# Loading q and k a batch ahead around the batch change of an attention and mixer kernel

## Chip, cores and metric

One core of one Trainium2 chip. The metric is the device time of one execution in microseconds (us). A profiled execution has a span some 1.8 us shorter than its time (434.77 us of time for 433.0 us of span).

## The reference, cut to what matters

```python
# q, k, v: (batch 8, heads 8, seq 576, head_dim 64), fp32
scores = scale * q @ k.transpose(0, 1, 3, 2) + bias[head]        # relative-position bias
attn   = exp(scores - max) ;  attn /= attn.sum(-1) + 1e-09
x      = (attn @ v) as (batch, seq, 512)                         # heads side by side
u      = x + ((x.T @ U) @ V).T                                   # low-rank mix over seq
out    = u + relu(u @ w_ch1) @ w_ch2                             # 512 -> 2048 -> 512
```

## The kernel before

Each batch is four *groups* (a pair of heads each), so there are 32, numbered 0 to 31; `g` is the group, `b` its batch, `pr` its slot in the batch. From group 4 on a group has three *thirds* (`seg`), each with score matmuls, the work of the pair before, and a ration of matmuls of an earlier batch's 512-2048-512 layer that fills TensorE's time. Scores need q and k with head_dim on the partitions. Batches 0 and 1 are transposed on TensorE; batches 2 to 7 are loaded by POOL as 128-row tiles (cast to bf16 on the way) and transposed by DMA, issued on SP, into `qkT[b % 2]`:

```python
    def hold(due, g, out, in_):
        held.append((due, g, lambda: nc.sync.dma_start_transpose(out=out, in_=in_)))

    def load_tasks(b, lag=2):                      # 15 items
        g0 = b * NPAIR
        def main(which, t):
            tl = load_main(b, which, t)            # POOL DMA
            if which < 2:                          # q, k: a transpose two thirds later
                hold(now[0] + lag, g0, qkT[b % 2][:, :, which, cols], tl)
        ...
        # order: remainder rows of q, k; q0 k0 q1 k1 q2 k2 q3 k3; remainder rows of v; v0..v3

    def emit_held(g, seg):                         # at the start of each third
        now[0] = 3 * g + seg
        ...                                        # at most two transposes that are due
...
    for g in range(NPAIR, NG):
        b, pr = divmod(g, NPAIR)
        for seg in range(3):
            emit_held(g, seg)
            ...                                    # scores of this third
            if seg == 1 and b < B - 1 and pr:
                if pr == 1:
                    pool_order += load_tasks(b + 1)
                # gate: POOL waits here until pair g - 1 is normalised
                nc.gpsimd.tensor_copy(out=gate, in_=x_pr[g - 1][0:1, 0, 0:2])
            if pr:
                for _ in range(3):
                    if pool_order:
                        pool_order.pop(0)()
            work.run(...)
            ...
```

So all 15 loads of the next batch, and ten transposes, fall into the last three groups of the batch before it. SP is one queue in order, and also carries the transposes of the mixer's input (`uT<-u_tok`) and the stores.

At the start, the four pairs of batch 0 come by plain loads in fp32: the first two pairs on SP and ScalarE, the third and fourth on SP at 10.9 to 14.6 us, between loads of the bias table. POOL casts the third, issues eight loads, and casts the fourth.

The softmax here doesn't subtract the row's maximum and nothing guards it: scores larger than these inputs give would overflow.

Of the kernel before, what the change touches and what calls it, by code (L numbers as in the profile page):

```python
# [35 lines left out]
def kernel(  # L36
# [12 lines left out]
    nc = tc.nc  # L49
    B, H, S, D = q.shape  # L50
# [9 lines left out]
    SP = 640  # L60
    S0 = 512
    P4W = 704
    NPAIR = H // 2
# [32 lines left out]
    gate = const.tile([1, 2], BF16)  # L96
# [4 lines left out]
    qkT = [const.tile([128, NPAIR, 2, SP], BF16, name=f"qkT{i}") for i in range(2)]  # L101
# [16 lines left out]
    def rem_heads(t):  # L118
        return t.rearrange("p (a two d) -> p a two d", two=2, d=D)
# [31 lines left out]
    def setup_gm():  # L151
        nc.vector.tensor_scalar(
            out=negt31, in0=tblT[:, 31:32], scalar1=-1.0, scalar2=None, op0=ALU.mult
        )
        nc.scalar.activation(gmT, tblT, AF.Exp, bias=negt31, scale=1.0)
# [69 lines left out]
    def first_load(which, h0, h1, st, dma):  # L225
        dma.dma_start(
            out=st.rearrange("p (h x) -> p h x", h=h1 - h0),
            in_=(q, k)[which][0, h0:h1, 0:S0, :].rearrange(
                "h (p j) d -> p h (j d)", j=4
            ),  # L230
        )

    def first_cast(st, cast):
        qb = qbp.tile([128, 512], BF16, name="qb")
        cast(  # L235
            out=qb.rearrange("p (j h d) -> p h j d", j=4, h=2),
            in_=st.rearrange("p (h j d) -> p h j d", h=2, j=4),
        )
        return qb

    def load_main(b, which, t):
        src = (q, k, v)[which]
        if which < 2:
            tl = qbp.tile([128, 512], BF16, name="qb")
            dst = tl.rearrange("p (h d) -> p h d", h=H)
        else:
            tl, dst = None, v_bf[b % 2][:, t, :, 0:64]
        nc.gpsimd.dma_start(  # L248
            out=dst,
            in_=src[b, :, t * 128 : (t + 1) * 128, :].rearrange("h p d -> p h d"),  # L250
        )
        return tl

    def load_pair(which, pr):
        tl = qbp.tile([128, 512], BF16, name="qb")
        dst = tl.rearrange("p (j h d) -> p j h d", j=4, h=2)
        for hh in range(2):
            nc.gpsimd.dma_start(  # L258
                out=dst[:, :, hh, :],
                in_=(q, k)[which][1, 2 * pr + hh, 0:S0, :].rearrange(  # L260
                    "(t p) d -> p t d", p=128
                ),
            )
        return tl

    def load_rem(b, which):
        src = (q, k, v)[which]
        vr = src[b, :, S0:S, :].rearrange("(a two) p d -> two p a d", two=2)
        if which < 2:
            dst = rem_heads(rem[b % 2][which])  # L270
        else:
            dst = v4_bf[b % 2].rearrange("p (a two) c -> p a two c", two=2)
        for par in range(2):
            rows = slice(par * 64, par * 64 + 64)
            nc.gpsimd.dma_start(out=dst[rows, :, par, 0:64], in_=vr[par])

    held = []
    now = [0]

    def hold(due, g, out, in_):  # L280
        held.append((due, g, lambda: nc.sync.dma_start_transpose(out=out, in_=in_)))  # L281

    def load_tasks(b, lag=2):
        g0 = b * NPAIR

        def main(which, t):
            tl = load_main(b, which, t)
            if which < 2:
                cols = slice(t * 128, (t + 1) * 128)
                hold(now[0] + lag, g0, qkT[b % 2][:, :, which, cols], tl)  # L290

        def remt(which):
            load_rem(b, which)
            if which < 2:
                src = rem[b % 2][which]
                hold(now[0] + lag, g0, qkT[b % 2][:, :, which, S0:SP], src)

        seq = [lambda which=which: remt(which) for which in range(2)]
        for t in range(NKT):
            for which in range(2):  # L300
                seq.append(lambda which=which, t=t: main(which, t))
        seq.append(lambda: remt(2))
        for t in range(NKT):
            seq.append(lambda t=t: main(2, t))
        return seq

    def load_uv():
        nc.gpsimd.dma_start(
            out=upad[:, 0:4, 0:R],
            in_=moe_U[0:S0, :].rearrange("(t p) r -> p t r", p=128),  # L310
        )
        for par in range(2):
            rows = slice(par * 64, par * 64 + 64)
            nc.gpsimd.dma_start(out=upad[rows, 4 + par, 0:R], in_=moe_U[S0:S, :])
        nc.gpsimd.dma_start(out=vpad[0:R, 0:S], in_=moe_V)

    def load_w1(ct):
        nc.gpsimd.dma_start(
            out=w1b[:, ct, :], in_=moe_w_ch1[ct * 128 : (ct + 1) * 128, :]
        )  # L320
# [187 lines left out]
    def band(g, kt):  # L508
        pr = g % NPAIR
        if kt < NKT:  # L510
            q0 = max(0, 128 * kt - 128)
            q1 = min(S, 128 * kt + 256)
            d0 = q0 - (128 * kt - 128)
            t = p_sb[g % 2][:, kt, :, q0:q1]
            e = eb[:, 2 * pr : 2 * pr + 2, d0 : d0 + q1 - q0]
        else:
            t = p4_sb[g % 2][:, 384:SP]
            e = eb4[:, pr, :]
        nc.vector.tensor_tensor(out=t, in0=t, in1=e, op=ALU.mult)  # L519
# [37 lines left out]
    x_pr = {}  # L557
# [61 lines left out]
    def mix_ut(g):  # L619
        mix_ut_ps(g)()  # L620
# [46 lines left out]
    qk0 = {}  # L667
    pool_cast = nc.gpsimd.tensor_copy
# [4 lines left out]
    q2, k2 = scratch[:, 1024:1536], scratch[:, 1536:2048]  # L673
    q3, k3 = scratch[:, 2048:2560], scratch[:, 2560:3072]
    first_load(0, 0, 2, q00, nc.sync)
    first_load(1, 0, 2, k00, nc.scalar)
    first_load(0, 2, 4, q1, nc.sync)
    first_load(1, 2, 4, k1, nc.scalar)
    nc.scalar.activation(gmT[:, 0:1], negt31, AF.Exp)
    setup_gm()  # L680
    setup_gp()
    load_eb(4)
    load_eb(0)
    first_load(0, 4, 6, q2, nc.sync)
    first_load(1, 4, 6, k2, nc.sync)
    load_eb(1)
    first_load(0, 6, 8, q3, nc.sync)
    first_load(1, 6, 8, k3, nc.sync)
# [11 lines left out]
    qk0[1] = [first_cast(x, nc.scalar.copy) for x in (q1, k1)]  # L700

    load_uv()
    load_rem(1, 0)
    load_rem(1, 1)
    qk0[2] = [first_cast(x, pool_cast) for x in (q2, k2)]
    qk1 = [[load_pair(which, 0) for which in range(2)]]
    for i in range(4):
        load_w1(i)
    qk0[3] = [first_cast(x, pool_cast) for x in (q3, k3)]
    load_rem(1, 2)  # L710
    for t in range(NKT):
        load_main(1, 2, t)
# [109 lines left out]
    pool_order = []  # L822
# [4 lines that stand above are left out]
            box = []  # L827
            if seg:
                main_scores(g, 2 * seg - 2)
            else:  # L830
                box = remainder_scores(g)
            if seg == 1 and b < B - 1 and pr:
                if pr == 1:
                    pool_order += load_tasks(b + 1)
                nc.gpsimd.tensor_copy(out=gate, in_=x_pr[g - 1][0:1, 0, 0:2])  # L835
            if pr:
                for _ in range(3):
                    if pool_order:
                        pool_order.pop(0)()
            work.run(1.85 if g < 2 * NPAIR + 2 else 2.2)  # L840
            for p in box:
                p()
            if g == NPAIR:
                if seg == 0:
                    pv(g - 1, 2)
                    pv(g - 1, 3)
                    normalise(g - 1)
                elif seg == 1:
                    mix_t(g - 1, nc.vector.tensor_copy)
                    mix_ut(g - 1)  # L850
                    ready[0] = True
                    work.run(1.5)
            elif seg == 0:
                if g > NPAIR + 1:
                    mix_h(g - 2)
            elif seg == 2:
                mix_t(g - 1, nc.scalar.copy)
            if seg == 0:
                band(g, 4)
                if NPAIR < g < 2 * NPAIR:  # L860
                    put_off.pop(0)()
                    put_off.pop(0)()
                if g > NPAIR:
                    pv_head(g - 1, 0)
            elif seg == 1:
                if g + 1 < 2 * NPAIR:
                    second_transposes(g + 1, qk1[g + 1 - NPAIR], 0)
                band(g, 0)
                band(g, 1)
                if g > NPAIR:  # L870
                    pv_head(g - 1, 1)
                if b > 1 and pr == 1:
                    ready[b - 1] = True
            else:
                if g + 1 < 2 * NPAIR:
                    second_transposes(g + 1, qk1[g + 1 - NPAIR], 1)
                band(g, 2)
                band(g, 3)
    g = NG - 1

    def last_rem(g):
# [46 lines left out]
```

## Time and profile before

| | before |
|---|---|
| time, first three runs | 431.82 us (431.15 to 433.02) |
| time of the run that was profiled | 434.77 us (span 433.0) |
| TensorE busy | 395.2 us, 91% |
| group length, undisturbed, from group 10 | 10.46 us |
| five batch changes (waiting group and the next) | 21.3 us above two undisturbed groups each |

The prediction shows the page's shares, the windows at the batch changes and the SP timeline. In the rows of a timeline, the time in square brackets is how long the engine stood idle before the instruction, and after the arrow stands what ended that.

### The profile page before, as it was taken

How to read it: one execution, taken by the hardware profiler on the slowest of the kernel's cores; microseconds unless marked ns; L12 is line 12 of the kernel's file. 1: busy time of each engine (PE TensorE's matmuls, PEld its weight loads, DVE VectorE, ACT ScalarE, POOL GpSimd, SP SyncE). 2: the span in 40 equal slices, each digit the busy share in tenths (PEclk: the TensorE clock that was granted, in tenths of full speed). 3: DMA queues.
4: the chain of work that ended last, by engine and by line, in shares of the span. 5: the costliest groups of instructions: out<-in, count | busy, mean ns of one | idle time of the engine just before them, and what ended most of it. 6: DMA issues, size and time to landing. Idle time of an engine off the chain costs nothing.

```text
span 433.0 us, 8998 instructions
## 1 busy us (share of the span) xinstructions
PE 395.2 (91%) x3620; PEld 212.7 (49%) x3620; DVE 241.4 (56%) x545; ACT 204.5 (47%) x283; POOL 126.7 (29%) x184
## 2 busy tenths in 40 slices
PE   2868988999969996999989998999699999999995
PEld 1545455555525553455545553555355554444442
DVE  5786877557715675356855674557455662331421
ACT  4867444566624554355545563456455651120310
POOL 8787475019200750038104810183000000000000
PEclk9899999999969999899999998999999999999998
DMA  9999999519961999139924993199812102101013
GB/s 152 227 182 141 144 161 156 116 55 140 141 64 62 110 124 139 39 74 157 155 38 75 174 134 53 54 138 159 85 38 69 44 15 63 58 2 73 26 24 73
DMA packets 167553, 42.56 MB, mean 98 GB/s; under 512 B 157232, under 2 KB 162392, under 8 KB 167512
## 3 DMA queue, kind: packets, MB, share of 16 engines
q0 software_dynamic: 108128, 17.39, 61.4%
q1 hardware_dynamic: 58840, 24.08, 28.9%
q8 instruction: 28, 0.46, 0.4%
q10 hardware_dynamic: 544, 0.52, 0.4%
q14 instruction: 13, 0.11, 0.1%
HBM read 37.84 MB, written 9.45 MB: 109 GB/s over the span
## 4 chain that ended last, share of the span: by engine, by line
PE 80%; DMA 8%; DVE 3%; SPq 3%; POOL 2%; issue 2%; ACT 1%; ACTq 0%; DVEq 0%
PE acc L356 30%; PE acc L341 26%; PE o L543 9%; PE sc L456 7%; DMA qkT<-qb 5%; SPq L281 2%; PE acc L579 2%; PE acc L595 2%; PE sc L469 2%; PE sc L490 1%; DMA g<-in_q_dram 1%; DMA tblT<-in_bias_table_dram 1%; POOL qb L235 1%; POOL qb L258 1%; DVE g L352 1%
## 5 line engine op out<-in xcount | busy, mean ns | idle before, releaser
L465 ACT ACTIVATE p_sb<-sc 128x1024 bf16<-128x1024 f32 x128 | 124.3, 1022 | 106.9 <-PE sc L456 106.6
L356 PE MATMUL acc<-w2b,g 128*128 128x512 bf16 x576 | 136.3, 387 | 0.0
L341 PE MATMUL acc<-uT,w1b 128*128 128x512 bf16 x512 | 121.2, 384 | 0.1
L356 PEld LDWEIGHTS <-g 128*128 128x128 bf16 x576 | 54.5, 99 | 73.1 <-issue 15.0
L341 PEld LDWEIGHTS <-w1b 128*128 128x128 bf16 x576 | 53.7, 98 | 72.7 <-issue 14.9
L352 DVE TENSOR_SCALAR g<-acc 128x512 bf16<-128x512 f32 x92 | 63.3, 690 | 44.0 <-PE acc L341 42.9
L519 DVE TENSOR_TENSOR p_sb<-p_sb,eb 128x768 bf16<-128x768 bf16 (+3 forms) x160 | 70.9, 467 | 12.9 <-ACT p_sb L465 12.2
L543 PEld LDWEIGHTS <-p_sb 128*128 128x128 bf16 x1600 | 55.8, 98 | 8.3 <-issue 2.0
L350 ACT ACTIVATE g<-acc 128x512 bf16<-128x512 f32 x52 | 31.1, 598 | 60.5 <-PE acc L341 44.2
L543 PE MATMUL o<-v_bf,p_sb 128*128 128x65 bf16 x1500 | 58.0, 193 | 0.0
L835 POOL COPY gate<-xp 1x2 bf16<-1x2 bf16 x18 | 3.2, 176 | 155.4 <-DVE xp L568 155.4
L366 DVE TENSOR_TENSOR ob<-acc,u_tok 128x512 f32<-128x512 f32 x32 | 22.1, 691 | 46.9 <-PE acc L356 46.6
L456 PE MATMUL sc<-qkT 64*128 64x512 bf16 x256 | 41.5, 392 | 1.4 <-ACT p_sb L482 0.6
L603 DVE TENSOR_TENSOR u_tok<-acc,xp 128x512 bf16<-128x512 f32 x32 | 22.0, 689 | 30.2 <-PE acc L595 30.0
L568 DVE TENSOR_TENSOR xp<-o,rcp 128x320 bf16<-128x320 f32 x60 | 29.5, 491 | 3.2
L469 PE MATMUL sc<-qkT 128*128 128x128 bf16 x128 | 14.4, 223 | 17.7 <-DMA qkT<-qb 13.8
L482 ACT ACTIVATE p_sb<-sc 128x512 bf16<-128x512 f32 x32 | 19.1, 597 | 24.2 <-PE sc L645 19.7
L248 POOL DMA_DIRECT2D v_bf<-in_v_dram x32 | 28.6, 912 | 4.7 <-PE acc L579 1.9
L248 POOL DMA_DIRECT2D qb<-in_k_dram x24 | 22.2, 923 | 3.0 <-issue 1.5
L248 POOL DMA_DIRECT2D qb<-in_q_dram x24 | 22.6, 940 | 0.3 <-DMA rem<-in_q_dram 0.3
L499 ACT ACTIVATE p_sb<-sc 128x640 bf16<-128x640 f32 x32 | 22.4, 699 | 0.1
L469 PEld LDWEIGHTS <-qkT 128*128 128x128 bf16 x128 | 8.9, 98 | 20.7 <-DMA qkT<-qb 15.2
(82 smaller groups left out, 250.2 us busy)
## 6 DMA issues: line engine op xcount, KB each, us to landing
out_dram<-ob SPq DMA_DIRECT2D x32, 256.0 KB, 2.0
v_bf<-in_v_dram POOLq DMA_DIRECT2D x32, 128.0 KB, 9.8
qb<-in_q_dram POOLq DMA_DIRECT2D x24, 128.0 KB, 5.5
qb<-in_k_dram POOLq DMA_DIRECT2D x24, 128.0 KB, 6.4
w1b<-in_moe_w_ch_dram POOLq DMA_DIRECT2D x4, 512.0 KB, 8.8
w2b<-in_moe_w_ch_dram POOLq DMA_DIRECT2D x4, 512.0 KB, 10.2
out_dram<-ob SPq DMA_DIRECT2D x8, 128.0 KB, 2.3
g<-in_q_dram SPq DMA_DIRECT2D x3, 256.0 KB, 6.3
```

The costliest lines, as they stand in the source:

```text
L248: nc.gpsimd.dma_start(out=dst, in_=src[b, :, t * 128 : (t + 1) * 128, :].rearrange("h p d -> p h d"),)
L341: nc.tensor.matmul(gp_, lhsT=w1b[:, ct, nt * 128 : (nt + 1) * 128], rhs=rhs[:, ct, :], start=(ct == 0), stop=(ct == 3),)
L350: nc.scalar.activation(g[:, nt, :], gp_, AF.Relu)
L352: nc.vector.tensor_relu(out=g[:, nt, :], in_=gp_)
L356: nc.tensor.matmul(op, lhsT=g[:, nt, tt * 128 : (tt + 1) * 128], rhs=w2b[:, nt, :], start=(nt == 0), stop=(nt == NHT - 1),)
L456: nc.tensor.matmul(sp[:, hh, :], lhsT=kT[rows, i * 128 : (i + 1) * 128], rhs=qT[rows, 0:S0], start=True, stop=True,)
L465: nc.scalar.activation(P[:, i, :, 0:S0], sp, AF.Exp, scale=scale)
L469: nc.tensor.matmul(sp[:, 0, kt * 128 : (kt + 1) * 128], lhsT=kT[:, kt * 128 : (kt + 1) * 128], rhs=qT[:, S0:SP], start=(kt == 0), stop=(kt ...
L499: nc.scalar.activation(P4[:, 0:SP], sp.rearrange("p a c -> p (a c)")[:, 0:SP], AF.Exp, scale=scale,)
L519: nc.vector.tensor_tensor(out=t, in0=t, in1=e, op=ALU.mult)
L543: nc.tensor.matmul(o[:, qt * 66 : qt * 66 + 65], lhsT=lhs[:, c0 : c0 + 128], rhs=rhs, start=(kt == NKT and qt == 0), stop=(kt == NKT - 1), ...
L568: nc.vector.tensor_tensor(out=xo[:, :, hh], in0=o[:, :, 0:64], in1=rbc, op=ALU.mult)
```

## The change

Its intent: take the transposes' landing off TensorE's path at each batch change. Loads of q and k begin a batch ahead (five items in the last slot of the batch before the last one, five in the next first slot), the transposes are due from the second slot's second third on, two a third, and v is loaded in the third slot. Batch 2, which cannot begin so early, gets five items in group 5 and ten in group 6. At the start the third pair's loads go to ScalarE's queue, and POOL casts pairs three and four ahead of the weights.

```diff
-    def load_tasks(b, lag=2):
+    def load_tasks(b):
         g0 = b * NPAIR
+        due = max(3 * (g0 - 3) + 1, now[0] + 2)
...
-                hold(now[0] + lag, g0, qkT[b % 2][:, :, which, cols], tl)
+                hold(due, g0, qkT[b % 2][:, :, which, cols], tl)
...
     first_load(1, 2, 4, k1, nc.scalar)
+    first_load(0, 4, 6, q2, nc.scalar)
+    first_load(1, 4, 6, k2, nc.scalar)
     nc.scalar.activation(gmT[:, 0:1], negt31, AF.Exp)
...
-    first_load(0, 4, 6, q2, nc.sync)
-    first_load(1, 4, 6, k2, nc.sync)
...
+    qk0[2] = [first_cast(x, pool_cast) for x in (q2, k2)]
     load_rem(1, 0)
     load_rem(1, 1)
-    qk0[2] = [first_cast(x, pool_cast) for x in (q2, k2)]
+    qk0[3] = [first_cast(x, pool_cast) for x in (q3, k3)]
+    load_w1(0)
+    load_w1(1)
     qk1 = [[load_pair(which, 0) for which in range(2)]]
-    for i in range(4):
-        load_w1(i)
-    qk0[3] = [first_cast(x, pool_cast) for x in (q3, k3)]
+    load_w1(2)
+    load_w1(3)
...
-            if seg == 1 and b < B - 1 and pr:
-                ...                                  (three items a third, as above)
+            if seg == 1 and g > NPAIR:
+                n = 0
+                if g == NPAIR + 1:
+                    pool_order += load_tasks(2)
+                    n = 5
+                elif g == NPAIR + 2:
+                    n = 10
+                elif pr == 3 and b < B - 2:
+                    pool_order += load_tasks(b + 2)
+                    n = 5
+                elif pr == 0 and b < B - 1:
+                    n = 5
+                elif pr == 2 and b < B - 1:
+                    n = 5
+                if n:
+                    nc.gpsimd.tensor_copy(out=gate, in_=x_pr[g - 1][0:1, 0, 0:2])
+                    for _ in range(n):
                         pool_order.pop(0)()
```

Source lines move by one after the first edit: L469 before is L470 after, L611 is L612.

More of the change, by code (lines that the diff above doesn't have):

```diff
@@ L295, in remt @@
                 src = rem[b % 2][which]
-                hold(now[0] + lag, g0, qkT[b % 2][:, :, which, S0:SP], src)
+                hold(due, g0, qkT[b % 2][:, :, which, S0:SP], src)
         seq = [lambda which=which: remt(which) for which in range(2)]
@@ L831 @@
                 box = remainder_scores(g)
-            if seg == 1 and b < B - 1 and pr:
-                if pr == 1:
-                    pool_order += load_tasks(b + 1)
-                nc.gpsimd.tensor_copy(out=gate, in_=x_pr[g - 1][0:1, 0, 0:2])
-            if pr:
-                for _ in range(3):
-                    if pool_order:
+            if seg == 1 and g > NPAIR:
[15 more added lines that the diff above has]
+                    for _ in range(n):
                         pool_order.pop(0)()
@@ L878 @@
                 band(g, 3)
+    assert not pool_order and not held
     g = NG - 1
```

## The prediction

> **What bounds the kernel now.** I read the page first (engine shares, slices), then the PE timeline around each batch change, then the windows over those stretches, then the SP and POOL timelines that feed them.
>
> ```profile
> PE 395.2 (91%) x3620; PEld 212.7 (49%) x3620; DVE 241.4 (56%) x545; ACT 204.5 (47%) x283; POOL 126.7 (29%) x184
> PE   2868988999969996999989998999699999999995
> PEclk9899999999969999899999998999999999999998
> DMA  9999999519961999139924993199812102101013
> ```
>
> TensorE is the bound: 91% busy, nothing else over 56%. So time can only come from TensorE's idle time (433.0 - 395.2 = 38 us) and from stretches at a lower clock. The idle time sits in the first slices and in single dents every fourth group, and each dent follows slices in which the DMA engines are full. The program works in groups (one pair of heads each, four to a batch, 0 to 31); inside the dents are the batch changes. The windows from the first score matmul of a batch to the last that had to wait (columns: length, PE busy, clock, DMA):
>
> ```profile
> core 0: us, PE busy (x), PEclk, DMA share, GB/s
> 120.66:124.84 4.18, 0.50 (x6) 0.79 1.06 106
> 168.90:173.30 4.40, 0.71 (x8) 1.00 1.27 151
> 216.79:218.35 1.56, 0.40 (x8) 1.00 0.63 120
> 259.86:262.44 2.58, 0.56 (x7) 1.00 0.99 163
> 305.63:309.57 3.94, 0.57 (x7) 1.00 1.25 117
> ```
>
> These are batches 3 to 7. In 16.7 us TensorE works 2.7, so about 13.9 us are waits. What they wait for, in the PE timeline, and what comes after, in the windows of the following group:
>
> ```profile
> 124.84 0.29 PE L469 MATMUL sc<-qkT 128*128 128x128 bf16 x1 [3.55 <-DMA qkT<-qb]
> ```
> ```profile
> 125.00:137.99 12.99, 12.99 (x108) 6.49 (x106) 5.48 (x13) 5.25 (x7) 0.00 (x0) 0.81 0.10 32
> 218.41:228.72 10.31, 10.31 (x106) 5.70 (x105) 6.38 (x14) 5.14 (x7) 0.00 (x0) 1.00 0.15 40
> 262.50:274.51 12.01, 12.01 (x107) 6.14 (x105) 5.74 (x13) 5.74 (x8) 0.00 (x0) 0.86 0.05 12
> ```
>
> The wait is for the last DMA transpose of k, and after three of the five (125, 173 and 262 us) TensorE runs a group at a mean clock of 0.81 to 0.86. Why the transpose is late, in the SP timeline:
>
> ```profile
> 105.02 9.98 SPq L281 DMA_TRANSPOSE qkT<-qb  x6
> 115.12 1.44 SPq L611 DMA_TRANSPOSE uT<-u_tok  x1
> 116.67 3.46 SPq L281 DMA_TRANSPOSE qkT<-qb  x2
> ```
>
> Six transposes take 10 us to issue and the last two go out at 116.7 to 120.1. In the trace's DMA records the loads of q, k and v of the same batch are issued from 96.3 to 111.5 us, the transposes from 99.7 to 120.1: both fight for the same engines, and k's last tile takes 9.9 us to land (105.2 to 115.1), its transposes 6 to 9.
>
> At the start, TensorE waits for the POOL casts of the fourth pair, which stand behind eight load issues:
>
> ```profile
> 24.89 0.40 PE L415 MATMUL acc<-ident,qb 128*128 128x128 bf16 x4 [1.50 <-POOL qb L235]
> 25.71 0.40 PE L415 MATMUL acc<-ident,qb 128*128 128x128 bf16 x4 [0.43 <-POOL qb L235]
> ```
>
> **What the Trainium skill says.** *DMA: Bandwidth & Descriptors*, "Issuing engines are not separate DMA queues": DMAs from scalar, sync and gpsimd run on the same 16 engines and interleave. The trace agrees: of the 128 KB loads after the gate at 95.7 us the first lands in 3.6 us, those issued beside transposes in 5 to 12. The same page, "Anatomy of one DMA": about 2.0 us plus bytes over 436 GB/s, so about 2.3 us for 128 KB. The trace's median for such a load is 5.5 to 9.8 us; the excess is queueing that the change can thin out. *TensorE: Matmul & The Clock Gate*, Part 1: an idle window of about 3.4 us, free-running, drops TensorE to half clock. The trace agrees roughly: the 3.55 us wait was followed by 6 us at 0.59, the 1.2 us wait at 218 by none; but waits of 0.65 and 1.36 us (262) were, and 2.23 and 1.13 us (309) were not, so the phase decides.
>
> **The change part by part.**
>
> (a) *Batch changes 3 to 7.* The order of instructions on TensorE and VectorE, with line numbers taken off, is identical in both kernels; ScalarE has two DMA issues more. So no work is added to the bound; only arrival times change. Loads of q and k move to the last group of the batch before the last one and the first group of the next; transposes run from the second slot's second third, two per third, five thirds long, with no load beside them but v's at the end. From group 10 on, the 13 undisturbed groups (start of the remainder score matmul to the next) average 10.46 us. The last two transposes then go out 7 us into the third group, which leaves 3.5 + 10.5 = 14 us before the next batch needs them. The worst landing of a transpose before is 9.8 us. I expect all five waits gone.
>
> Worth: group pairs (waiting group plus next) last 27.38, 26.82, 22.19, 24.92, 24.58 us against 20.92, so 6.5, 5.9, 1.3, 4.0 and 3.7: 21.3 us together. As a cross-check, groups 10 to 31 start 240.97 us apart; 21 times 10.46 is 219.6, so 21.4. Of it 13.9 are waits, and 5.9 clock (12.99 x 0.19 + 12.22 x 0.14 + 12.01 x 0.14). As the waiting and the slow groups are wholly TensorE-bound, all of it is on the path: **-21.4 us**.
>
> (b) *Batch change 2 gets tighter.* It had no wait before (81.93 us). Before, all but k's last tile were loaded behind the first gate (53 us); now five items are, and k1, q2, k2, q3, k3 wait for the gate at 65.3, with v behind them and batch 3's first five at 77. At 0.88 us of issue each k3 goes out at about 69 and lands 5 to 6 us later, 75; its transpose is held behind the uT transpose (75.1) as before, issues at about 77.7 and lands 2.4 us later undisturbed, 4 to 6 us with v beside it: 80 to 84, needed at 82. I put **+1.0 us** (0 to 3) on a new wait there.
>
> (c) *Start.* The third pair's loads leave SP at 10.9 us for ScalarE at about 1.7, the fourth's move about 1 us forward, and the POOL casts of both go ahead of w1. TensorE waits 1.50 + 0.43 = 1.9 us at the fourth pair's transposes. But VectorE is busy right up to 25.18 and the copy that follows the transposes stood at 26.14 after 0.96 idle, so only about 1.0 can be kept. The third pair's transposes (19.22) had no wait in front, so its earlier cast gives nothing. Against: 0.5 MB more competes with the first pair in the first 8 us. **-1.0 us** (-2.5 to +0.5).
>
> (d) *POOL gates, tail:* more gates, 0.18 us each on an engine at 29%: nothing. From 358 us on TensorE runs back to back: unchanged.
>
> Sum: 431.8 - 21.4 + 1.0 - 1.0 = **410.4 us**, 5% less.
>
> **Rivals.**
>
> R1: the wait moves. A load a batch ahead collides with the uT transposes or the stores, both on SP's queue in order; or batch 2's wait is large and cools the clock. For: SP is one queue, and (b) is tight. Against: steady groups have the DMA engines nearly idle half the time (0.05 to 0.15 in the windows above), and TensorE never waited for uT. It would give back 3 to 8 us: 413 to 418.
>
> R2: the waits hide something else: with q and k there in time, ScalarE or VectorE becomes the bound after a batch change, so only part of 21 us comes back. For: ScalarE's first exponent of a batch follows at once. Against: batch 5's change, nearly unhindered, was followed by a full-rate 10.31 us group with VectorE 6.38 and ScalarE 5.14. It would give 415 to 420.
>
> R3: only the clock stays bad, from short gaps elsewhere: 416.
>
> R4: the start gains more (all of 1.9 us and earlier bias tables): 408.
>
> **Range and chances.** (a) is a sum of measured waits on an unchanged TensorE program: 18 to 22. With (b) 0 to 3 and (c) -2.5 to +0.5, the ends are about 405 and 417. Faster by over 2% needs under 423.2; all rivals stay below it, so 0.97. Within 2%: 0.025; slower would need a stall that nothing shows: 0.005.
>
> **What would show it right or wrong.** Right: the slices keep no dent after the first five but perhaps one at group 8; "PE sc L469 <- DMA qkT<-qb" falls from 13.8 us to under 3; the clock row is 9 throughout after the start; loads and transposes no longer overlap; group spacing is 10.3 to 10.5 us throughout. (b) shows as a wait before the first score matmul of group 8, near 81 us. (c) shows as the start of group 4's first score (47.93) at 46 to 48. Wrong: a wait of TensorE on uT or ob, groups longer than 10.6 us, or waits that return at batches 3 to 7.

## The result, and the profile after

| | before | after |
|---|---|---|
| median of four runs | 432.42 us (431.15 to 433.47) | 414.47 us (414.35 to 416.87) |
| span profiled | 433.0 us | 412.7 us |

The ratio is 0.9599 (95% interval 0.9554 to 0.9645): 4.0% faster. Ratios here are the mean time of one kernel's fast runs over that of the other's of the same rounds, so not quite the ratio of the medians.

The page of the changed kernel, in the rows that answer to those of the prediction:

```profile
PE 384.8 (93%) x3557; PEld 211.4 (51%) x3620; DVE 241.2 (58%) x545; ACT 204.4 (50%) x283; POOL 126.0 (31%) x183
...
PE   1888898899999999999999999999999999999995
...
PEclk9999999999999999999999999999999999999999
DMA  9999999998999499979996899699011002102013
```

The dents at every fourth group are gone, the clock row shows 9 in every slice, and the DMA row, which swung between 9 and 1 from one batch change to the next, stays at 4 or more through the first 28 slices. Of TensorE's slices only some of the first eight, up to batch 2's change, and the last are still below 9. Over the 21 groups from group 10 to 31, the windows of before and then of after (columns: length; busy time of PE, PEld, DVE, ACT, POOL; clock; DMA share; GB/s):

```profile
100.02:340.98 240.96, 227.05 (x2200) 122.92 (x2197) 139.69 (x309) 125.08 (x172) 70.03 (x99) 0.97 1.06 100
```
```profile
101.29:320.69 219.40, 217.19 (x2158) 121.13 (x2197) 139.79 (x309) 124.98 (x172) 64.20 (x91) 1.00 0.95 104
```

The same work takes 219.40 us, not 240.96: 21.6 us less. TensorE's idle time there falls from 13.9 to 2.2 us, and its busy time by 9.9 us: 5.9 of that is the slow clock, and part of the rest (at most the 2.2 us that are left idle) may be only that the trace after lacks more matmul records (2158 stand where 2200 do before). VectorE and ScalarE did the same work in both.

The lines of what uses `qkT`, before and then after (idle time of TensorE's matmuls and weight loads added together, times it happened; then the transposes' time from issue to landing):

```profile
  DMA qkT<-qb: 29.0, 17
DMA to landing us min/median/max: 2.4/7.4/9.8
```
```profile
  DMA qkT<-qb: 3.6, 2
DMA to landing us min/median/max: 2.3/3.0/6.9
```

The median landing falls from 7.4 to 3.0 us. The one wait that is left stands at batch 2, in the PE timeline after:

```profile
81.23 0.33 PE L470 MATMUL sc<-qkT 128*128 128x128 bf16 x3
83.28 0.23 PE L470 MATMUL sc<-qkT 128*128 128x128 bf16 x1 [1.71 <-DMA qkT<-qb]
```

Group 7 lasts 12.46 us where it lasted 10.46 before. From batch 3 on, SP's timeline shows how early the transposes are now:

```profile
97.46 2.54 SPq L281 DMA_TRANSPOSE qkT<-rem  x2
...
100.74 5.16 SPq L281 DMA_TRANSPOSE qkT<-qb  x4
...
107.30 2.08 SPq L612 DMA_TRANSPOSE uT<-u_tok  x1
109.48 5.19 SPq L281 DMA_TRANSPOSE qkT<-qb  x4
```

The last leaves at 114.7 us and lands at 118.4; batch 3 needs it at 122.0. The same margin is 3.4 us at batch 5 and 4.2 us at batch 6; for batches 4 and 7 the trace does not tell the last landing, but neither waits.

### The profile page after: what moved, and what is told of

Its sections match the earlier page's. It is cut to its first block, busy times and chain, and to the rows that moved or that the text cites. A ratio compares the mean times of both kernels' runs of the same rounds, so it can differ in the third digit from the quotient of the medians.

```text
span 412.7 us, 8928 instructions
## 1 busy us (share of the span) xinstructions
PE 384.8 (93%) x3557; PEld 211.4 (51%) x3620; DVE 241.2 (58%) x545; ACT 204.4 (50%) x283; POOL 126.0 (31%) x183
## 4 chain that ended last, share of the span: by engine, by line
PE 88%; DVE 3%; DMA 3%; issue 2%; ACT 2%; SPq 0%; POOL 0%; ACTq 0%
PE acc L342 30%; PE acc L357 29%; PE o L544 11%; PE sc L457 8%; PE acc L580 2%; PE sc L470 2%; PE acc L596 2%; DMA rem<-in_q_dram 2%; PE sc L491 2%; DMA qkT<-qb 1%; ACT p_sb L466 1%; DVE xp L569 1%; DVE qkT L421 1%; PE acc L445 1%; DVE qkT L447 0%
## 5 line engine op out<-in xcount | busy, mean ns | idle before, releaser
L357 PE MATMUL acc<-w2b,g 128*128 128x512 bf16 x545 | 128.3, 379 | 1.6 <-issue 0.2
L342 PE MATMUL acc<-uT,w1b 128*128 128x512 bf16 x484 | 115.7, 380 | 1.8 <-issue 0.3
L520 DVE TENSOR_TENSOR p_sb<-p_sb,eb 128x768 bf16<-128x768 bf16 (+3 forms) x160 | 69.9, 461 | 12.7 <-ACT p_sb L466 12.2
L483 ACT ACTIVATE p_sb<-sc 128x512 bf16<-128x512 f32 x32 | 19.1, 597 | 10.5 <-PE sc L646 5.5
L567 DVE RECIPROCAL rcp<-o 128x5 f32<-128x5 f32 x60 | 11.5, 191 | 13.8 <-PE o L544 13.3
L470 PE MATMUL sc<-qkT 128*128 128x128 bf16 x128 | 13.0, 224 | 4.5 <-DVE qkT L447 1.8
```

Of the source, the lines that this page charges most:

```text
L342: nc.tensor.matmul(gp_, lhsT=w1b[:, ct, nt * 128 : (nt + 1) * 128], rhs=rhs[:, ct, :], start=(ct == 0), stop=(ct == 3),)
L357: nc.tensor.matmul(op, lhsT=g[:, nt, tt * 128 : (tt + 1) * 128], rhs=w2b[:, nt, :], start=(nt == 0), stop=(nt == NHT - 1),)
L520: nc.vector.tensor_tensor(out=t, in0=t, in1=e, op=ALU.mult)
```

## The experiments

Each of the three jobs runs the kernel before on the same chip, 11 times, from 430.7 to 442.2 us. A run over 1.5% above the fastest of its kernel is put down as slow and left out of the ratios; on one core nothing else tells that state, so long waits can earn the label too. The medians of the fast runs (8, 11 and 9 of 11) are 433.95, 434.95 and 434.10 us. Waiting group means the group ahead of a batch change.

**The changed kernel again.** No edit.

> The changed kernel itself again, as the measure for the other runs of this chip. Its first profile spans 412.7 us and its times are 1.76 us more than its spans, so 414.5 us. The kernel before is run beside it; its profile on record was its slowest run (434.8 us against 431.2 to 433.5 for the others). If that run merely had larger batch-change waits than usual, the gain in the medians is 2 to 3 us below the 20.3 us that separate the two profiles, so about 17.5 to 18.5 us; if the chip of the first result was at fault, the gain here is 20 us or more.

Measured: 415.26 us (413.06 to 416.73, six runs), ratio 0.9555 (0.9502 to 0.9608). The gain in the medians of fast runs, 18.7 us, lies just above the first figure and below the second. The fast runs of the kernel before spread from 430.7 to 436.4 us here, so its first three runs (431.8) lie towards its fast end. The profiled run was the slowest, and shows one way in which the changed kernel still moves by 4 us: batch 2's wait was longer, and a slow clock followed. Its PE timeline, and the window of the following group:

```profile
83.89 0.23 PE L470 MATMUL sc<-qkT 128*128 128x128 bf16 x1 [3.17 <-DMA qkT<-qb]
```
```profile
84.07:95.17 11.10, 10.89 (x100) 6.02 (x101) 5.88 (x13) 5.10 (x7) 4.55 (x6) 0.85 1.01 94
```

Group 7 took 13.92 us and group 8 11.10 against 9.43 in the other profile: 5.1 us in all for batch 2.

**Only the batch-ahead part.**

```diff
  # changed kernel, start undone
-    first_load(0, 4, 6, q2, nc.scalar)      # ahead of the table load
-    first_load(1, 4, 6, k2, nc.scalar)
+    first_load(0, 4, 6, q2, nc.sync)        # after load_eb(0)
+    first_load(1, 4, 6, k2, nc.sync)
  # and POOL's order as before: k2's cast after load_rem(1, 1), k3's after load_w1(3)
```

> Only the batch-ahead loads and transposes, the start as before. If the parts are independent and the start is worth what group 4's first score shows (47.93 before, 47.23 after: 0.7 us), this is 0.7 us slower than the changed kernel, about 415.2 us. If the start part does more than that (through the order of w1 and the pair loads), it is 1.5 us or more slower; if the start part is worth nothing, equal within 0.3 us.

Measured: 415.27 us (413.24 to 416.62), ratio 0.9569 (0.9517 to 0.9621), against 415.26 and 0.9555 for the whole change. The start is worth nothing that these times can show (the two intervals are 0.5% wide to each side, 2 us); all of the gain that they can show is in the batch-ahead part.

**Only the start.**

```diff
  # kernel before, with the start of the changed kernel
+    first_load(0, 4, 6, q2, nc.scalar)      # ahead of the table load
+    first_load(1, 4, 6, k2, nc.scalar)
-    first_load(0, 4, 6, q2, nc.sync)        # after load_eb(0)
-    first_load(1, 4, 6, k2, nc.sync)
  # and POOL's new order
```

> Only the new start, the batch changes as before. Independent parts: 0.7 us faster than the kernel before, with waits for the transposes of q and k at batches 3 to 7 of 10 to 14 us in its profile and none at batch 2. If the start shifts the phase of the waits against the clock's window, it can come out anywhere within 2 us of the kernel before, and its profile will show a different set of slow-clock groups.

Measured: 433.14 us (429.35 to 438.51) with two slow runs, 431.94 us for the four fast ones, ratio 0.9953 (0.9885 to 1.0021): the same. Its profile (only its waits are read) has 15.1 us of waits for `qkT` in nine matmuls, a little over the 10 to 14 expected. One of them, 0.19 us, is at batch 2, where none was expected.

**Loads ahead, transposes late.**

```diff
-        due = max(3 * (g0 - 3) + 1, now[0] + 2)
+        due = max(3 * (g0 - 2), now[0] + 2)
```

> Loads a batch ahead as in the changed kernel, but the transposes of batches 3 to 7 due two slot thirds later, where the kernel before had them (from the start of the third group to the second third of the fourth). Theory 1, sharing: the transposes were late because loads and transposes were in flight together; alone they land 2.4 us after issue, so the last is there 2 to 3 us before it is needed, and the time is that of the changed kernel plus 0 to 5 us (the next batch's first loads begin beside the last two transposes). Theory 2, lateness: they were late because they were issued late; then the waits of batches 3 to 7 come back to 10 us or more and the time is 428 us or more.

Measured: 416.57 us (415.45 to 419.29), ratio 0.9611 (0.9547 to 0.9675; the record's class is "unclear"). Lateness of issue alone falls: the transposes are issued at nearly the times of before (last one at 116.9 to 118.3 us for batch 3, before 118.9 to 120.1) and the five waiting groups last 11.82, 10.40, 10.54, 10.54 and 11.35 us where they lasted 14.37, 14.62, 11.88, 12.91 and 14.04. The landings now (median 4.5 us, before 7.4):

```profile
DMA to landing us min/median/max: 2.4/4.5/6.6
```

But two of the five changes still waited (1.3 us at batch 3, 0.9 us at batch 7), and at batch 5 the last transpose landed at 205.45 us for a need at 205.7: the transposes are on the edge here. In the changed kernel they are not.

**The whole sequence a slot earlier, still overlapping.**

```diff
+            first = 1 if b == 1 else 0
-            if seg == 1 and b < B - 1 and pr:
-                if pr == 1:
+            if seg == 1 and b < B - 1 and pr >= first:
+                if pr == first:
                     pool_order += load_tasks(b + 1)
...
-            if pr:
+            if pr >= first:
```

> The kernel before, with the whole interleaved sequence for batches 3 to 7 (loads of q, k, v with transposes two slot thirds behind) begun one slot earlier, still overlapping. Batch 2 and the start as before. If distance is enough: loads and transposes still land 5 to 12 us after issue, because they share, but there are 10.5 us more of slack against waits of at most 4.4 us, so no wait at batches 3 to 7, 10.5 us or less per group throughout, and about 412 to 415 us. If the overlap itself hurts (TensorE or the filler's transposes held up by it), the groups with the overlap are longer than 10.6 us and the time is 418 us or more.

Measured: 422.07 us (420.67 to 422.51), ratio 0.9687 (0.9640 to 0.9733): neither prediction in full. Distance removes all five waits at the batch changes (those groups last 10.33 to 10.54 us), although the landings are as slow as before:

```profile
DMA to landing us min/median/max: 2.3/7.6/9.4
```

But the time did not follow, because a new wait stands in group 9. SP's and PE's timelines there, and the windows:

```profile
94.13 1.29 SPq L611 DMA_TRANSPOSE uT<-u_tok  x1
```
```profile
102.69 2.72 PE L341 MATMUL acc<-uT,w1b 128*128 128x512 bf16 x6 [4.99 <-DMA uT<-u_tok]
```
```profile
96.00:103.00 7.00, 1.70 (x8) 0.51 (x6) 1.21 (x4) 2.33 (x3) 4.36 (x6) 0.90 2.41 124
103.00:108.00 5.00, 4.78 (x20) 2.50 (x20) 1.56 (x3) 2.16 (x4) 0.87 (x1) 0.50 1.68 184
```

The mixer's input for batch 1, `uT`, is transposed at 94.1 us amid the new traffic and lands only at 102.6 (2.3 us from issue when it is alone, 84.9 us); the 512-2048-512 layer of that batch begins with it. TensorE stands 5.0 us, then runs 5 us at half clock; group 9 lasts 15.22 us, not 8.40, and group 10 11.64, not 10.54: 7.9 us. This is the wait that takes the place of the one removed, in a version other than the one under study. It happened once, where TensorE had little else to do: in the trace before, group 9 lasts 8.40 us (in all other kernels too), its second third holds a single matmul of batch 0's layer (95.29 us), and those of batch 1's begin at 97.56 us.

**Only v's loads moved, in the kernel before.**

```diff
+            if seg == 2 and pr == 0 and 1 < b < B - 1:
+                nc.gpsimd.tensor_copy(out=gate, in_=x_pr[g - 1][0:1, 0, 0:2])
+                for task in load_tasks(b + 1)[10:]:
+                    task()
             if seg == 1 and b < B - 1 and pr:
                 if pr == 1:
-                    pool_order += load_tasks(b + 1)
+                    pool_order += load_tasks(b + 1)[: 10 if b > 1 else 15]
```

> The kernel before, with only the loads of v for batches 3 to 7 taken out of the sequence, to the last third of the first slot, ahead of q and k. If v's traffic is what delays the last transposes of q and k, the last of them is issued at 3.6 to 5 us into the fourth group and lands 3 us later, before it is needed, and nearly the whole gain is here: 414 to 418 us. If q and k loads beside their own transposes are enough to make them late, the waits of batches 3 to 7 stay at half or more (7 us of 13.9 in the profile) and the time is 423 us or more.

Measured: 414.76 us (414.13 to 419.27), ratio 0.9555 (0.9490 to 0.9620): as large a gain as that of the whole change, with four lines added and one altered. SP's timeline, and the landings:

```profile
104.82 9.57 SPq L281 DMA_TRANSPOSE qkT<-qb  x6
115.81 3.19 SPq L281 DMA_TRANSPOSE qkT<-qb  x2
```
```profile
DMA to landing us min/median/max: 2.3/5.0/8.1
```

The last two transposes are issued less than 2 us earlier than before (115.8 against 116.7 us; done at 119.0 against 120.1). But all that was issued ahead of them has landed by 116.9, so the last lands 2.5 us after issue, at 120.11, not 5.9 us after it, at 124.8: of the 4.7 us gained, 1.4 are earlier issue and 3.3 a shorter landing. Batch 3 needs it at 120.1 to 120.3: just in time. Four changes have no wait, the fifth (batch 7) 1.6 us; one of the four runs took 419.27 us and was not profiled, so this version is on the edge too. Its sum is also not made up like that of the change: batch 2 has no wait here. Together with the run of late transposes this says what was wrong before: too much in flight in the last 25 us ahead of the change. Taking out q and k's loads is nearly enough, and so is taking out v's.

**Batch 2: ten items in group 5.**

```diff
-                    n = 5          # group 5
+                    n = 10
-                    n = 10         # group 6
+                    n = 5
```

> The changed kernel, but all ten items of q and k of batch 2 behind the first gate and only v behind the second. In the changed kernel the group before batch 2 lasted 12.46, 13.92 and 11.73 us in three profiles against 10.46 before, with a slow-clock group after the second. If k's late loads are the cause: 10.5 to 11.2 us here and 1.5 to 3 us less time than the changed kernel, so 412 to 413.5 us. If the first loads of batch 3, which run beside the last transposes, are the cause, it stays at 11.7 us or more.

Measured: 412.46 us (411.97 to 413.40), ratio 0.9473 (0.9437 to 0.9510): the time fits the first of the two cases expected, but group 7 still lasts 11.75 us in the profile (the slowest of the six runs), with a wait of 1.0 us, which fits the second. k's last tile now lands at 71.1 us, not at 74.7, yet the last transpose leaves at 77.4 us as in the changed kernel (77.7), held by its delay of two thirds behind the `uT` transpose. It lands at 82.1 beside batch 3's first loads, and is needed at 81.1. So k's late loads were not the only cause. The trace before settles it further: there the last transpose left at 77.7 us too and landed at 80.1, 2.4 us later, with neither v's loads nor batch 3's in flight any more; in the changed kernel it took 5.5 us beside both.

**Batch 2: the same, and transposes one third after.**

```diff
-        due = max(3 * (g0 - 3) + 1, now[0] + 2)
+        due = max(3 * (g0 - 3) + 1, now[0] + 1)
```

> As the run with the ten items, and batch 2's transposes due one slot third after their loads, not two, so that the last two leave before the uT transpose of the seventh group. The last lands some 3 us earlier than there, so both causes are out of the way: 10.46 us for the group before batch 2, 2 to 3.5 us less than the changed kernel, 411.5 to 413 us, and less spread from run to run. If the queue now waits for loads in flight and holds up the uT transposes, groups 5 or 6 get longer than 11.66 and 11.88 us.

Measured: 412.31 us (411.85 to 412.90), ratio 0.9469 (0.9433 to 0.9506). The profile spans 410.4 us; group 7 lasts 10.46 us, groups 5 and 6 11.66 and 11.87 as everywhere. The last transpose leaves at 75.0 us and lands at 80.2, 0.7 us before the first of these scores. In the PE timeline batch 2's scores begin without a gap:

```profile
80.88 0.39 PE L470 MATMUL sc<-qkT 128*128 128x128 bf16 x4
```

Run again on another chip:

> The run with batch 2's ten items and the shorter delay again, so that the two mends stand on one chip: 412.3 us there, the same within 0.7 us here; no wait for the transposes of q and k at any batch.

Measured: 412.21 us (411.77 to 412.64), ratio 0.9496 (0.9463 to 0.9529), and no wait for `qkT`. In both jobs the spread is about 1 us, against 3.7 us for the changed kernel in its job of six runs. That points to batch 2's wait as most of what the changed kernel varied by. How much each of the two edits does is not separated: the run with the first alone was not slower (412.46 us).

**The start: third pair's loads later on ScalarE.**

```diff
-    first_load(0, 4, 6, q2, nc.scalar)
-    first_load(1, 4, 6, k2, nc.scalar)
     nc.scalar.activation(gmT[:, 0:1], negt31, AF.Exp)
     setup_gm()
+    first_load(0, 4, 6, q2, nc.scalar)
+    first_load(1, 4, 6, k2, nc.scalar)
```

> The changed kernel, but ScalarE issues the third pair's two loads after its table load and the exponents of the bias table, at about 4.9 us and not at 1.7. In the changed kernel TensorE waited 1.16 us at 8.96 us for the remainder rows of q, whose loads landed at 8.8 us against 7.6 before: if the two loads beside them are the cause, that wait goes, batch 1's first remainder score (mean 37.4 us over six profiles with the new start, 38.1 over four with the old) moves to 36.3 to 37, and the time falls 0.5 to 1 us. If the third pair's later arrival or a later cast of the first pair on ScalarE takes it back, no change or slower.

Measured: 414.09 us (412.22 to 417.63), ratio 0.9555 (0.9505 to 0.9604), against 0.9555 for the changed kernel in another job. The cause named was right: the first remainder score is at 9.9 to 10.2 us in all seven profiles with the new start, at 9.2 to 9.3 in the four with the old one, and at 9.24 here. Here is the wait in the changed kernel and then in this one:

```profile
8.96 0.61 PE L427 MATMUL acc<-ident,rem 128*128 128x128 bf16 x2 [1.16 <-DMA rem<-in_q_dram]
```
```profile
8.26 0.26 PE L427 MATMUL acc<-ident,rem 128*128 128x128 bf16 x1 [0.18 <-DMA rem<-in_k_dram]
```

But batch 1's first remainder score was at 37.6 us in this profile, not under 37, so the time won did not last to there (in the next run, which has the same start, it was at 37.0). The profiled run, 416.93 us, again had a long wait and a slow clock at batch 2 (groups 7 and 8: 13.5 and 11.1 us), so the fall of 0.5 to 1 us that was expected could not show in these times. **With batch 2's mend:**

> Both mends together: batch 2's q and k behind the first gate with transposes one third after, and the third pair's loads issued later. If they add, the profile spans 409.5 to 410 us (410.4 with batch 2 alone) and the time is 411 to 412 us, below the kernel before and the changed kernel in all rounds.

Measured: 412.59 us (411.62 to 413.70), ratio 0.9510 (0.9471 to 0.9549), beside 412.21 us without this edit on the same chip, although the one profile is the shortest of all (409.8 us). The two mends do not add in the times. The version that beats both kernels is the one with batch 2 mended alone: about 5% under the kernel before, and 2 to 3 us under the changed kernel by the medians of separate jobs.

## Why the prediction was right or wrong

The time was inside the range. The predicted 410.4 us is 4.1 us below the 414.5 measured: 3.0 of it from the base, 1.0 from (b), 0.3 from (c), less 0.2 from (a). The lower end of the range was mis-added: the parts as given make 407.3 to 417.3 us, not 405 to 417. Step by step:

- *(a) Batch changes 3 to 7, -21.4 us:* right. All five waits went, and groups 10 to 31 take 21.6 us less. That the order of work on TensorE is the same in both kernels let the sum of waits and slow groups be carried over. Two supports were weaker than stated. The last transposes leave at 112.2 to 114.7 us, not 7 us into the third group (108), since SP issues them after `uT_rem` and `uT` and v's loads slow them: batch 3's margin was 3.6 us, not the most of 14. And "no load beside them but v's" counted v as harmless, while the run with v moved shows that, in the kernel before, v's loads alone made the difference between late and just in time.
- *(b) Batch 2, +1.0 us (0 to 3):* the place was right and the times worked out came true (k's last tile issued at 68.6 us and landed at 74.7, its transpose issued at 77.7 and landed at 83.2). The term was too small: 2.0 us in the first profile (12.46 against 10.46), 1.3 in that of the batch-ahead part alone and 5.1 in that of the first repeat, where a slow clock followed the wait. That last is rival R1's second form, seen; the profiled runs of 416.73 us (changed kernel) and 416.93 us (with the start edited) both had it. The two edits of batch 2 together take the wait away. What made it is the traffic beside the last transpose, not its issue: it left at 77.7 us before and after, and landed 2.4 us later before, 5.5 after. The prediction had this landing among its cases (2.4 us undisturbed, 4 to 6 beside v); batch 3's first loads it named without counting them.
- *(c) Start, -1.0 us:* -0.7 us in the profile pair (47.93 to 47.23 us), and 0.65 us between the means of the four profiles with the old start and the seven with the new. The score at 47.93 us that the prediction called group 4's is group 5's; group 4's moved by the same 0.7. The loss allowed for, more traffic in the first 8 us, was real: a wait of 1.16 us at 8.96 us. In the times of the separate parts, neither alone nor on top does the start show anything beyond their intervals, which are 2 to 3 us to each side, so times neither confirm nor refute the 0.7 us.
- *The base:* the step that failed, and most of the miss. Waits were measured in a profile of a 434.77 us run, and taken off a median of 431.82 us; waits read in one run belong to the time of that run. 434.77 with the predicted terms is 413.4, and with the measured ones (-21.6, +2.0, -0.7) 414.5. With 33 more runs the kernel before has medians of 434.0 to 435.0 us in its fast runs, so the profile was typical and the first three times were fast. That just these waits are what varies in the kernel before is likely and not shown: only one run of it was profiled.
- *Rivals:* R2 (another engine becomes the bound) is refuted by full-rate groups of 10.3 to 10.5 us throughout; R3 by the clock row; R4 by the start's 0.7 us in the profiles. R1's first form, a wait on `uT`, did not come in the changed kernel but did in the version that merely began a slot earlier, 5.0 us and half clock after it.
- *Tests:* the wait line was to fall below 3 us: 1.7 us in the first profile, 3.2 in the second. Loads and transposes were no longer to overlap: v's still do, without a wait.

The slow clock can be read more closely than the prediction did. In every trace the granted clock changes only on a grid of 3.41 us steps (before: half clock from 123.09, 174.29 and 263.04 us, which lie 15 and 41 steps after the first), and a half-clock stretch inside the run lasts one or two steps. Here are the steps that ended batch 6's and batch 7's waits in the trace before, each with the step after it (length; PE busy; clock; DMA share; GB/s):

```profile
259.63:263.04 3.41, 1.39 (x15) 1.00 0.86 134
263.04:266.45 3.41, 3.41 (x10) 0.50 0.02 5
307.41:310.83 3.42, 1.55 (x10) 1.00 0.39 77
310.83:314.24 3.41, 3.41 (x43) 1.00 0.00 0
```

Batch 6's two waits fell into one step and left TensorE idle for 2.02 us of it, and the next step ran at half clock. Batch 7's longer ones straddled two steps, idle for 1.50 and 1.87 us, and no slow step followed. Over all thirteen profiles, from 25 us on, every full-clock step with 1.93 us or more of idle TensorE was followed by half clock, and none with 1.87 us or less was. This is the phase that the prediction spoke of, and tells the waits that a slow clock followed from those that none did.

What stays open: that count is over traces, and no experiment moved a wait across the grid. Nor do the runs say by which rule loads and transposes share the DMA engines.

## What to carry to other kernels

When a transfer is late, look at everything in flight beside it before moving it: here the loads of v, needed last, made q and k late, and moving those alone gave as much as the whole change. Moving all traffic to an earlier place can land it on another transfer that something waits for at once. And take a sum of waits off the time of the run that was profiled, not off the median of others. Whether a wait cost clock too shows in TensorE's idle time in each step of the clock's grid, not in the longest gap.

## What the Trainium skill lacked or had wrong

- *DMA: Bandwidth & Descriptors*, "DMA Transpose (X-bar)": gives constraints, and the page elsewhere a bandwidth, but no time from issue to landing. These runs show 2.3 us alone for a 128x512 bf16 SBUF transpose and up to 9.8 us beside loads from POOL, and about 1.2 us of SP's queue for each issue, up to 3.0 us then. All results were right with transposes beside ordinary loads; the time suffered: the kernel before lost 21.3 us around its five batch changes.
- The same page, "Anatomy of one DMA": its fit gives an estimate of 2.3 us for the 128 KB that a load writes (2.6 us for the 256 KB that it reads). These loads (fp32 to bf16, in runs of 256 bytes) took 3.4 us with little beside them (issued at 88.2 us in the changed kernel), 5 to 12 us among others. Elsewhere the page calls such short runs slow, but it has no time for them.
- *TensorE: Matmul & The Clock Gate*, Part 1 and its rule on idle gaps over about 3.4 us: shorter gaps were enough here, and the length of a gap did not decide. Waits of 0.65 and 1.36 us (batch 6, before) were followed by a group at a clock of 0.86, those of 2.23 and 1.13 us (batch 7) by one at 1.00. A grid of 3.41 us steps agrees with the page's free-running window, but the window need not be idle throughout: half clock followed 1.93 us of idle in it, but not 1.87 us. The page tells of short idle spells that do it, too, without a figure.
